# Other tokens for the first expert pass, and unsplit float32 keys for the first query tile, in a fused attention and expert kernel

## The chip, the cores and the metric

The program runs on one core of one Trainium2 chip. The metric is the device time of one execution in microseconds (us); the time before is the median of three executions. The trace is that of one profiled execution; "us" in it counts from the span's start.

## The reference

Three stages follow each other: attention with a learned relative bias, a layer of four gated experts, and a gated product layer. Cut to what matters:

```python
# q, k, v: (batch 2, heads 8, positions 576, head width 64), float32
scores = q @ k.T / 8 + bias[h, i, j]      # bias: a 1-32-8 network of log1p|i-j| / log1p(i)
attn = softmax(scores); x = attn @ v      # -> x: (1152 tokens, 512)
for e in range(4):                        # domain_probs, normalised, are the gates p
    out += p[:, e:e+1] * (relu(x @ w1[e]) @ w2[e])      # 512 -> 1024 -> 512
a = out @ w_a; b = out @ w_b              # 512 -> 1536
result = (a * b) @ w_out                  # 1536 -> 512
```

A score row of position i needs the bias rows of that position alone; the expert layer works token by token.

## The kernel before

**The order.** No instruction order is written by hand. The code declares operations with a cost on each engine, a rank and the buffers that they hold (`op`, lines 99 to 124). A planner (`Plan.run`, lines 137 to 223) plays them through with these costs and emits each engine's instructions in the order in which it would have begun them. On TensorE it prefers attention (rank 0) and fills the rest with expert products (rank 2, "fill"). On the chip every engine then runs its own list strictly in that order and waits on semaphores. All loads and stores go through SyncE's one queue, in order too.

**Precision.** Most products are done in a reduced float32 format of one TensorE pass. An operand x is split: hi is x rounded to that format, lo is x - hi. Three products hi*hi, hi*lo, lo*hi stand for one. For scores the key tile holds the same 64 rows twice, hi in partitions 0 to 63 and lo in 64 to 127 (`kcast`, `ksub`), so that two products (with qh and with ql, line 490) cover the sum. Other products (bias network, transposes, attention times values) are plain float32.

**Bias.** 36 groups of 16 positions (`bias_group`, line 347): per group three rectified tiles `hh` on VectorE (line 356) and one on ScalarE (358), four products into `pb` (370), a shift and a mirror into one of three buffers `bst` (388, 395), and a store to the DRAM table `bias_d` (405). A score step loads its 128 rows back as the tile `bt` (458), after the stores of all rows that it needs have landed.

**Attention.** The 576 positions are five query tiles t = 0 to 4 (four of 128, one of 64). A *step* is one head pair m (four of them), one batch b and one tile t, made of two *score units*, one for each head: the products `ps` (490), the sum with the bias and its row minimum on VectorE (`L493`), the exponential on ScalarE (503), transposes `pt` (516, 533), and their copies into `ptb`. A *group* is one or more steps of a head pair, closed by `values` (546): the reciprocal of the row sums, its spread `rp`, the product with the values `pv` (581), `xf` (587), and the split into `x_hi` and `x_lo`. The groups before are: tile 0 of batch 0 for each m, tile 1 of batch 0 for each m, tiles 0 and 1 of batch 1, then tiles 2 to 4 of both batches (lines 415 to 417). Keys are loaded and split by `inputs` (429) once for tiles 0 and 1 and once more for tiles 2 to 4, 16 times in all.

**Score buffers.** There are two PSUM buffers for `ps` and four for `pt`, `rp` and `pv` until the seventh group has ended (`experts_begin`, 1010). From then on there are one and two, and the others serve the experts.

**Experts.** The first pass of the experts (`w1_item`, line 724, with the products `up` of line 708; `w2_item`, 739, with `pz` of line 719) takes tokens 0 to 255 of the token order, the second pass the other 896. In each pass there are 32 weight units of 512 KB, loaded, cast and split (`unit`, 615). The first 256 tokens are batch 0's tiles 0 and 1 (`X[0, 0]`, line 730), so the first pass can begin when the first eight groups are done; the second pass begins when the attention has ended. After that come the products of the last stage (line 842), in which no part of the attention is left.

Of the kernel before, what the change touches and what calls it, by code (L numbers as in the profile page):

```python
# [19 lines left out]
P = 128  # L20
# [9 lines left out]
C0 = 256  # L30
CW = (C0, S - C0)
BW = 2 * S
# [12 lines left out]
SPLIT = True  # L45
# [181 lines left out]
def tile_kernel(ctx, tc, qd, kd, vd, cst, probs, w1r, w2r, war, wbr, wor, out):  # L227
# [56 lines left out]
    W2 = CW[1]  # L284
    place(R["q2"], ap_, "q2", 1, [P, 2, W2])
    place(R["q"], ap_, "q", 2, [P, 2, W2], F32R, pair=True)
# [4 lines left out]
    place(R["ptb"], ap_, "ptb", 2, [P, 9, W2])  # L291
    place(R["pr"], ap_, "pr", 3, [P, 2, S])
    place(R["rb"], ap_, "rb", 2, [P, W2])
    place(R["xf"], ap_, "xf", 2, [P, W2])
# [7 lines left out]
    place(R["h1"], mid, "h", 2, [P, 2, C0], F32R, pair=True)  # L302
# [116 lines left out]
    QK, fins, guests = {}, [], []  # L419
# [9 lines left out]
    def inputs(m, b, c):  # L429
        w = CW[c]  # L430
        q2, k2 = new("q2"), new("k2")
        if (b, c) == (0, 0) and m >= 2:
            d = slice(2 * m - 4, 2 * m - 2)
            k = Buf(t=x_hi[:, d, C0:C0 + S])
            q = Buf(t=tuple(x_lo[:, d, C0 + z * C0:2 * C0 + z * C0] for z in range(2)))
        else:
            k, q = new("k"), new("q")
        op({"SP": 440}, lambda e: nc.sync.dma_start(out=q2.t[:, :, :w], in_=qd[m, b][:, :, C0 * c:C0 * c + w]), w=[q2], size=P * 8 * w)
        op({"SP": 440}, lambda e: nc.sync.dma_start(out=k2.t, in_=kd[m, b]), w=[k2], size=P * 8 * S)
        op(t_copy(2 * w, ENGINES["qcast"]), lambda e: copy(e, q.t[0][:, :, :w], q2.t[:, :, :w]), r=[q2], w=[q], prio=RANK["prep"], lock=True)  # L440
        op(t_two(2 * w, ENGINES["qsub"]), lambda e: engine[e].tensor_tensor(out=q.t[1][:, :, :w], in0=q2.t[:, :, :w], in1=f(q.t[0][:, :, :w]), op=ALU.subtract), r=[q2], rw=[q], prio=RANK["prep"], lock=True)
# [27 lines left out]
    def step(m, b, t, k, q0, Q, K, ptb, sums):  # L469
# [3 lines left out]
        for s in range(2):  # L473
# [67 lines left out]
        else:  # L541
            for s in range(2):
                rr = slice(s * D, (s + 1) * D)
                op(t_psum(64, ENGINES["tail"]), lambda e, s=s, rr=rr: copy(e, ptb.t[rr, 8, 256:320], tail.t[rr, s * D:(s + 1) * D]), r=[tail], w=[ptb])

    def values(m, b, ts, w, V, ptb, sums):
# [12 lines left out]
        def spread(e):  # L559
            for t in range(full):  # L560
                nc.tensor.transpose(rp.t[:, t * P:t * P + P], rx.t[:, t].rearrange("p s d -> p (s d)"), ident)
            if 4 in ts:
                nc.tensor.transpose(rp.t[:, n:n + P], sums.t[:, 4:5].to_broadcast([P, P]), ident)
# [20 lines left out]
        c = int(ts[0] > 1)  # L584
# [532 lines left out]
```

## Time and profile before

| what | value |
|---|---|
| median of three executions | 833.38 us (832.92 to 834.51) |
| profiled execution: span from the first to the last instruction | 829.8 us |
| median less that span | 3.6 us |
| TensorE busy in the span | 802.7 us (97%) |
| VectorE busy in the span | 627.3 us (76%) |
| ScalarE busy in the span | 352.5 us (42%) |

The span is that of the profiled execution; its own time outside the span is not recorded, so the 3.6 us between it and the median of the other executions stand for what lies around it. "Busy" is the union of an engine's recorded instructions; TensorE's are pipelined and overlap, so the start of one to the start of the next is the cost in a dense stretch, not its duration. "Idle before" names what ended the idle time in front of an instruction.

### The profile page before, as it was taken

The page shows a single profiled execution, that of the slowest core. Times are in us where ns is not written, and L with a number is a line of the kernel's source. Part 1 is how long each engine was busy: PE and PEld are TensorE (multiplying, and loading weights), DVE is VectorE, ACT ScalarE, POOL GpSimd, SP SyncE. Part 2 cuts the span into 40 slices and gives each one's busy share as a digit, 9 for nine tenths or more (in the row PEclk, how much of TensorE's full clock was granted, in tenths as well). Part 3 has the DMA queues.
Part 4 walks back from the last instruction along what each step waited for, and adds up shares of the span by engine and source line. Part 5 has one row for each costly group of instructions (what it writes and reads, how often), then busy time and mean ns, then how long its engine had stood idle before and what let it go on. Part 6 is the DMA issues. An engine that isn't in the chain of part 4 may idle for free.

```text
span 829.8 us, 12737 instructions
## 1 busy us (share of the span) xinstructions
PE 802.7 (97%) x4859; PEld 668.8 (81%) x4859; DVE 627.3 (76%) x1232; ACT 352.5 (42%) x696; POOL 43.5 (5%) x62
## 2 busy tenths in 40 slices
PE   7778999999999999999999999999999999999997
PEld 2446776898897788889888988888888999899996
DVE  7998999788888768787888787875556665747545
ACT  6677877477676611132122212213345432323211
POOL 1002100000110000000000000000010001100000
PEclk9999999999999999999999999999999999999999
DMA  6989877575656444556465555640302221211103
GB/s 225 311 286 355 280 242 249 195 238 189 222 176 213 131 164 120 185 176 206 115 199 194 164 141 169 224 126 2 101 1 87 67 66 37 77 31 47 51 2 114
DMA packets 48589, 128.13 MB, mean 154 GB/s; under 512 B 5136, under 2 KB 9488, under 8 KB 48528
## 3 DMA queue, kind: packets, MB, share of 16 engines
q1 hardware_dynamic: 48384, 127.18, 47.5%
q8 instruction: 38, 0.62, 0.3%
q14 instruction: 23, 0.19, 0.1%
q10 hardware_dynamic: 144, 0.13, 0.0%
HBM read 101.46 MB, written 25.84 MB: 153 GB/s over the span
## 4 chain that ended last, share of the span: by engine, by line
PE 90%; DVE 5%; DMA 3%; ACT 1%; issue 1%; DVEq 0%
PE pz L719 32%; PE up L708 24%; PE pw L842 9%; PE ps L490 5%; PE pv L581 4%; PE pr L842 4%; PE pt L516 4%; PE pq L842 2%; PE pb L370 2%; DMA k<-in_kd 1%; DVE hh L356 1%; PE pz L922 1%; DMA bt<-bias_d 1%; ACT pr L503 1%; DMA bias_d<-bst 1%
## 5 line engine op out<-in xcount | busy, mean ns | idle before, releaser
L719 PE MATMUL pz<-wh,hh 128*128 128x512 f32 x386 | 154.0, 399 | 0.0
L719 PE MATMUL pz<-wl,hh 128*128 128x512 f32 x386 | 152.3, 395 | 0.0
L719 PE MATMUL pz<-wh,hl 128*128 128x512 f32 x386 | 151.6, 393 | 0.0
L708 PE MATMUL up<-x_hi,wh 128*128 128x256 f32 (+2 forms) x384 | 133.1, 347 | 0.4 <-DVE hl L736 0.4
L708 PE MATMUL up<-x_hi,wl 128*128 128x256 f32 (+2 forms) x384 | 129.8, 338 | 0.0
L708 PE MATMUL up<-x_lo,wh 128*128 128x256 f32 (+2 forms) x384 | 129.7, 338 | 0.0
L735 ACT ACTIVATE hh<-up 128x256 fp32r<-128x256 f32 (+2 forms) x96 | 47.1, 491 | 141.7 <-PE up L708 141.2
L234 ACT CAST wh<-wst 128x1024 fp32r<-128x1024 f32 (+1 forms) x66 | 66.4, 1007 | 91.0 <-PE pz L719 71.4
L719 PEld LDWEIGHTS pz<-wl,hh 128*128 128x128 f32 x386 | 72.5, 188 | 17.2
L619 DVE TENSOR_TENSOR wl<-wst,wh 128x1024 fp32r<-128x1024 f32 x64 | 78.0, 1222 | 9.9 <-ACT wh L234 9.6
L719 PEld LDWEIGHTS pz<-wh,hh 128*128 128x128 f32 x386 | 72.6, 188 | 15.0 <-issue 0.7
L719 PEld LDWEIGHTS pz<-wh,hl 128*128 128x128 f32 x386 | 72.6, 188 | 14.7
L708 PEld LDWEIGHTS up<-x_hi,wh 128*128 128x128 f32 x384 | 72.4, 188 | 9.5 <-issue 1.6
L708 PEld LDWEIGHTS up<-x_lo,wh 128*128 128x128 f32 x384 | 72.4, 189 | 6.5
L708 PEld LDWEIGHTS up<-x_hi,wl 128*128 128x128 f32 x384 | 72.3, 188 | 5.9
L736 DVE SCALAR_TENSOR_TENSOR hl<-up,hh 128x256 fp32r<-128x256 f32 (+2 forms) x96 | 53.0, 554 | 29.3 <-ACT hh L735 28.8
L234 ACT COPY ct<-pw 128x512 f32<-128x512 f32 (+3 forms) x48 | 27.8, 579 | 108.0 <-PE pw L842 100.6
L493 DVE CUSTOM_DVE_ANT_0 pr<-ps,bt 128x576 f32<-128x576 f32 (+1 forms) x80 | 59.7, 754 | 10.9 <-PE ps L490 8.4
L503 ACT ACTIVATE pr<-pr,sums 128x576 f32<-128x576 f32 x72 | 55.9, 776 | 12.5 <-DVE sums L493 11.7
L370 PE MATMUL pb<-hh,cs 128*32 128x288 f32 (+17 forms) x352 | 46.6, 497 | 6.6 <-DVE hh L356 5.1
L356 DVE TENSOR_SCALAR hh<-cs,negb 128x576 f32<-128x576 f32 (+17 forms) x108 | 49.1, 504 | 0.2
L516 PE MATMUL pt<-ident,pr 128*128 128x128 f32 x288 | 43.6, 280 | 2.6 <-ACT pr L503 2.4
(161 smaller groups left out, 1415.6 us busy)
## 6 DMA issues: line engine op xcount, KB each, us to landing
wst<-in_w1r SPq DMA_DIRECT2D x32, 512.0 KB, 4.1
wst<-in_w2r SPq DMA_DIRECT2D x32, 512.0 KB, 4.3
bt<-bias_d SPq DMA_DIRECT2D x24, 576.0 KB, 5.7
bias_d<-bst SPq DMA_DIRECT2D x36, 295.5 KB, 4.7
k<-in_kd SPq DMA_DIRECT2D x16, 576.0 KB, 4.9
v<-in_vd SPq DMA_DIRECT2D x20, 320.0 KB, 4.9
s<-in_war SPq DMA_DIRECT2D x12, 512.0 KB, 5.1
wz_d<-hl SPq DMA_DIRECT2D x24, 256.0 KB, 2.5
```

The costliest lines, as they stand in the source:

```text
L234: (nc.scalar.copy if e == "ACT" else engine[e].tensor_copy)(out, in_)
L356: op({"DVE": n / 1.92 + 240}, lambda e, hh=hh, G=G: nc.vector.tensor_scalar(out=hh.t[:, :n], in0=tab[:, :n], scalar1=sc[:, G:G + 1], scala ...
L370: nc.tensor.matmul(t[32 * g:32 * g + 32, o + lo:o + hi], w2s, hs[g].t[:, lo:hi], start=True, stop=True)
L493: nc.vector.tensor_tensor_reduce(out=pr.t[r0:r1, c].rearrange("p (a b) -> p a b", a=2), in0=ps.t[r0:r1, :, :HS], in1=bt.t[r0:r1, c].rearra ...
L503: nc.scalar.activation(out=pr.t[:, c], in_=pr.t[:, c], func=AF.Exp, scale=-1.0, bias=sums.t[:, neg:neg + 1], accum_out=sums.t[:, col:col + 1])
L516: nc.tensor.transpose(pt.t[:, kt * P:kt * P + P], pr.t[:, s, k0:k0 + P], ident)
L619: op(t_two(1024, ENGINES["wlo"]), lambda e: engine[e].tensor_tensor(out=w.t[1], in0=wst.t, in1=f(w.t[0]), op=ALU.subtract), r=[wst], rw=[w ...
L708: nc.tensor.matmul(u.t[:, :n], a[:, d, ft * P:(ft + 1) * P], x[:, d, lo:lo + n], start=(d == 0 and j == 0), stop=(d == 3 and j == 2))
L719: nc.tensor.matmul(z.t, a[:, ft, tt * P:(tt + 1) * P], bb[:, ft, :], start=(first and ft == 0 and j == 0), stop=(final and ft == 1 and j = ...
L735: relu = op({"ACT": n / 1.2 + 170}, lambda en, ft=ft, u=u: nc.scalar.activation(out=h.t[0][:, ft, :n], in_=u.t[:, :n], func=AF.Relu), r=[u ...
L736: op({"DVE": n / 0.96 + 160}, lambda en, ft=ft, u=u: nc.vector.scalar_tensor_tensor(out=h.t[1][:, ft, :n], in0=u.t[:, :n], scalar=0.0, in1 ...
L842: nc.tensor.matmul(o_, s[:, k], d[:, k], start=(first and k == 0 and i == 0), stop=(k == 1 and i == 2), skip_group_check=True)
```

## The change

The first 256 tokens of the token order become query tile 0 of batch 0 and query tile 0 of batch 1. The groups become: tile 0 of both batches for each m (8 groups), then for each m tiles 1 and 2 of both batches, then tiles 3 and 4 of both. For tile 0 the scores are plain float32: the keys lie in a new array `kf` once, with head width in the partitions and the two halves of the 576 positions in partitions 0 to 63 and 64 to 127, and a unit is two products, one for each half (`qk_plain`). Neither keys nor queries are cast or split there. For the other tiles keys are loaded and split once for each head pair and batch (`keys`), 8 times in all, and queries for each group (`queries`). The raw key buffer `k2` becomes two, the split key buffer `k` three.

```diff
-C0 = 256
+C0 = P
+GW = (256, 320)
+X0 = B * C0
+QW = 2 * P
...
-    place(R["k2"], ap_, "k2", 1, [P, 2, S])
-    place(R["k"], ap_, "k", 2, [P, 2, S], F32R)
+    place(R["k2"], ap_, "k2", 2, [P, 2, S])
+    place(R["k"], ap_, "k", 3, [P, 2, S], F32R)
...
-    groups = [(m, 0, (t,)) for t in range(2) for m in range(NM)] if SPLIT else [(m, 0, (0, 1)) for m in range(NM)]
-    groups += [(m, 1, (0, 1)) for m in range(NM)]
-    groups += [(m, b, (2, 3, 4)) for m in range(NM) for b in range(B)]
+    groups = [(m, b, (0,)) for m in range(NM) for b in range(B)]
+    groups += [(m, b, ts) for m in range(NM) for ts in ((1, 2), (3, 4)) for b in range(B)]
...
-    def inputs(m, b, c):
...
+    def plain(m):
+        k2, q2 = new("k2"), new("q2")
+        op({"SP": 440}, lambda e: nc.sync.dma_start(out=k2.t.rearrange("p b n -> p (b n)"), in_=kf[m]), w=[k2], size=P * 8 * S)
+        for b in range(B):
+            op({"SP": 440}, lambda e, b=b: nc.sync.dma_start(out=q2.t[:, b].rearrange("p (s w) -> p s w", s=2), in_=qd[m, b][:, :, :P]), w=[q2], size=P * 8 * P)
+        return k2, q2
+
+    def keys(m, b):
+        k2, k = new("k2"), new("k")
         op({"SP": 440}, lambda e: nc.sync.dma_start(out=k2.t, in_=kd[m, b]), w=[k2], size=P * 8 * S)
         op(t_copy(2 * S, ENGINES["kcast"]), lambda e: copy(e, k.t, k2.t), r=[k2], w=[k], prio=RANK["prep"], lock=True)
         op(t_two(2 * S, ENGINES["ksub"]), lambda e: engine[e].tensor_tensor(out=k.t[D:P], in0=k2.t[D:P], in1=f(k.t[D:P]), op=ALU.subtract), r=[k2], rw=[k], prio=RANK["prep"], lock=True)
-        return q, k
+        return k
...
+            def qk_plain(e, s=s, ps=ps):
+                for half in range(2):
+                    r = slice(half * D, half * D + D)
+                    nc.tensor.matmul(ps.t[:, half, :HS], Q.t[r, b, s * P:s * P + P], K.t[r, b, s * HS:s * HS + HS], start=True, stop=True)
+
+            op({"PE": 640}, qk_plain, r=[Q, K, bt], w=[ps], hold=[pr, sums]) if t == 0 else op({"PE": 560 if len(runs) == 2 else 700}, qk, r=[Q, K, bt], w=[ps], hold=[pr, sums])
...
-        xs = [X[0, 0]] if p == 0 else list(X.values())[1:]
+        xs = [X[b, p] for b in range(B)]
```

**Where it moves instructions.** VectorE, between the bias groups, ahead of the first score sums (`hh` are the rectified tiles, whose width falls by 16 from group to group; `k`, `x_hi` and `x_lo` are places of split keys and queries). Before:

```order
L356 TENSOR_SCALAR hh<-cs,negb 128x464 x3
L443 TENSOR_TENSOR k<-k_210,k 64x1152
L356 TENSOR_SCALAR hh<-cs,negb 128x448 x2
L234 CAST x_lo<-q_259 128x2x256
L356 TENSOR_SCALAR hh<-cs,negb 128x448
L441 TENSOR_TENSOR x_lo<-q_259,x_lo 128x2x256
L356 TENSOR_SCALAR hh<-cs,negb 128x432 x3
```

The changed kernel:

```order
L357 TENSOR_SCALAR hh<-cs,negb 128x464 x3
L357 TENSOR_SCALAR hh<-cs,negb 128x448 x3
L357 TENSOR_SCALAR hh<-cs,negb 128x432 x3
L357 TENSOR_SCALAR hh<-cs,negb 128x416 x3
L357 TENSOR_SCALAR hh<-cs,negb 128x400 x3
```

Every cast and split of keys and queries has left this stretch; the first score sum follows the same 42 `hh` tiles as before.

TensorE, around the first expert product `up`. Before, where 22 score units stand ahead of it:

```order
L581 MATMUL pv<-ptb,v 64x128 x10
L516 MATMUL pt<-ident,pr 128x128 x4
L533 MATMUL pt<-ident,pr 128x128
L490 MATMUL ps<-k,qh 128x288 x2
L490 MATMUL ps<-k,ql 128x288 x2
L561 MATMUL rp<-ident,rx 128x128 x2
L370 MATMUL pb<-hh,cs 32x400 x4
L490 MATMUL ps<-k,qh 128x288 x2
L490 MATMUL ps<-k,ql 128x288 x2
L708 MATMUL up<-x_hi,wh 128x256
```

The changed kernel, where 18 units stand ahead (16 of tile 0, two of tile 1):

```order
L371 MATMUL pb<-hh,cs 32x320 x4
L589 MATMUL pv<-ptb,v 64x128 x10
L524 MATMUL pt<-ident,pr 128x128 x4
L371 MATMUL pb<-hh,cs 32x336 x4
L524 MATMUL pt<-ident,pr 128x128 x4
L541 MATMUL pt<-ident,pr 128x128
L589 MATMUL pv<-ptb,v 64x128 x10
L371 MATMUL pb<-hh,cs 32x352 x4
L722 MATMUL up<-x_hi,wh 128x256
```

The expert products now come after the products of 22 bias groups instead of 25, and 36 of them stand in a row there.

TensorE, where the first expert pass ends (`pz` is its second product; `up` of 384 columns is the second pass). Before:

```order
L719 MATMUL pz<-wl,hh 128x512
L516 MATMUL pt<-ident,pr 128x128 x4
L535 MATMUL pt<-ident,pr 128x128
L536 MATMUL pt<-ident,pr 64x128
L561 MATMUL rp<-ident,rx 128x128 x2
L563 MATMUL rp<-ident,sums 128x128
L581 MATMUL pv<-ptb,v 64x320 x10
L708 MATMUL up<-x_hi,wh 128x384
```

The changed kernel:

```order
L733 MATMUL pz<-wl,hh 128x512
L495 MATMUL ps<-k,qh 128x288 x2
L495 MATMUL ps<-k,ql 128x288 x2
L524 MATMUL pt<-ident,pr 128x128 x4
L543 MATMUL pt<-ident,pr 128x128
L544 MATMUL pt<-ident,pr 64x128
L495 MATMUL ps<-k,qh 128x288 x2
L495 MATMUL ps<-k,ql 128x288 x2
L569 MATMUL rp<-ident,rx 128x128
L571 MATMUL rp<-ident,sums 128x128
L524 MATMUL pt<-ident,pr 128x128 x4
```

Before, one `pv` is left to do after the last `pz` of the first pass; now 20 of the 80 score units, with their transposes and six `pv`, come after it. From the first `up` of 384 columns on, TensorE's two lists are the same.

## Rows read from the trace of the kernel before

**Rows 1.** The page's head, and its busy time by engine.

```profile
span 829.8 us, 12737 instructions
PE 802.7 (97%) x4859; PEld 668.8 (81%) x4859; DVE 627.3 (76%) x1232; ACT 352.5 (42%) x696; POOL 43.5 (5%) x62
```

**Rows 2.** Stretches: length, busy us by engine (instructions), clock, DMA share, GB/s.

```profile
0.00:31.39 31.39, 23.03 (x136) 6.46 (x136) 25.79 (x54) 20.10 (x30) 4.01 (x15) 1.00 0.72 232
31.39:80.00 48.61, 39.00 (x346) 27.36 (x345) 45.83 (x130) 36.18 (x82) 4.23 (x5) 0.96 0.95 337
...
91.33:279.00 187.67, 187.23 (x1375) 153.73 (x1374) 161.21 (x328) 130.53 (x276) 12.68 (x15) 1.00 0.66 212
279.00:293.84 14.84, 13.36 (x90) 8.77 (x88) 9.88 (x20) 8.51 (x20) 0.88 (x1) 1.00 0.41 136
```

**Rows 3.** The line of the expert products: shortest, median, longest ns; first and last start.

```profile
L708 PE MATMUL up<-x_hi,wh x384: 277/336/481, 91.3 to 596.7; 128*128 128x256 f32 x64, 128*128 128x384 f32 x64, 128*128 128x512 f32 x64
```

**Rows 4.** VectorE by line, 4.2 to 33.4 us: busy, mean ns, idle before.

```profile
L356 DVE TENSOR_SCALAR hh<-cs,negb 128x576 f32<-128x576 f32 (+13 forms) x42 | 19.4, 521 | 0.1
L443 DVE TENSOR_TENSOR k<-k,k 64x1152 fp32r<-64x1152 f32 x2 | 2.7, 1355 | 1.4 <-ACT k L234 1.3
L441 DVE TENSOR_TENSOR ql<-q,qh 128x512 fp32r<-128x512 f32 x2 | 1.4, 686 | 0.0
L234 DVE CAST qh<-q 128x512 fp32r<-128x512 f32 x2 | 0.8, 424 | 0.0
L234 DVE CAST x_hi<-k 128x1152 fp32r<-128x1152 f32 x1 | 0.8, 759 | 0.2 <-DMA k<-in_kd 0.2
```

**Rows 5.** SyncE's queue in order of time: start, length, transfer, count.

```profile
22.12 1.39 SPq L405 DMA_DIRECT2D bias_d<-bst  x2
27.96 0.89 SPq L458 DMA_DIRECT2D bt<-bias_d  x2
```

**Rows 6.** Transfers issued from 8 to 32 us: size, median us to landing.

```profile
bias_d<-bst SPq DMA_DIRECT2D x10, 295.5 KB, 4.1
bt<-bias_d SPq DMA_DIRECT2D x3, 576.0 KB, 5.1
```

**Rows 7.** VectorE in order of time: start, length, instruction, idle before.

```profile
33.43 0.74 DVE L493 CUSTOM_DVE_ANT_0 pr<-ps,bt 128x576 f32<-128x576 f32 x1
34.10 0.08 DVE L493 DVE_READ_ACCUMULATOR2_ANT sums<- 128x1 f32 x1
...
35.06 0.76 DVE L493 CUSTOM_DVE_ANT_0 pr<-ps,bt 128x576 f32<-128x576 f32 x1 [0.21 <-PE ps L490]
...
36.71 0.67 DVE L234 COPY ptb<-pt 128x512 f32<-128x512 f32 x1
...
43.98 1.20 DVE L356 TENSOR_SCALAR hh<-cs,negb 128x352 f32<-128x352 f32 x3
...
46.08 1.22 DVE L619 TENSOR_TENSOR wl<-wst,wh 128x1024 fp32r<-128x1024 f32 x1
...
65.66 0.76 DVE L493 CUSTOM_DVE_ANT_0 pr<-ps,bt 128x576 f32<-128x576 f32 x1 [1.56 <-DMA bt<-bias_d]
```

**Rows 8.** TensorE in order of time, early, and the values' product of a long group.

```profile
38.71 1.31 PE L490 MATMUL ps<-x_hi,x_lo 128*128 128x288 f32 x8
39.95 1.31 PE L581 MATMUL pv<-ptb,v 128*64 128x128 f32 x20
...
45.09 1.42 PE L370 MATMUL pb<-hh,cs 128*32 128x368 f32 x16
...
280.20 2.91 PE L581 MATMUL pv<-ptb,v 128*64 128x320 f32 x20
```

**Rows 9.** TensorE in order of time, the attention's end.

```profile
288.73 0.66 PE L516 MATMUL pt<-ident,pr 128*128 128x128 f32 x4 [0.43 <-ACT pr L503]
...
290.52 0.44 PE L561 MATMUL rp<-ident,rx 128*128 128x128 f32 x2 [0.91 <-ACT ptb L234]
...
293.84 0.44 PE L708 MATMUL up<-x_hi,wh 128*128 128x384 f32 x1
```

More of the change, by code (lines that the diff above doesn't have):

```diff
@@ L226, in tile_kernel @@
 @with_exitstack
-def tile_kernel(ctx, tc, qd, kd, vd, cst, probs, w1r, w2r, war, wbr, wor, out):
+def tile_kernel(ctx, tc, qd, kd, kf, vd, cst, probs, w1r, w2r, war, wbr, wor, out):
     nc = tc.nc
@@ L301, in tile_kernel @@
     place(R["wst"], right, "wst", 2, [P, 1024])
-    place(R["h1"], mid, "h", 2, [P, 2, C0], F32R, pair=True)
+    place(R["h1"], mid, "h", 2, [P, 2, X0], F32R, pair=True)
     new = lambda z, name=None: Buf(R[z], None, name or z)
@@ L442, in inputs, with queries @@
         op(t_copy(2 * S, ENGINES["kcast"]), lambda e: copy(e, k.t, k2.t), r=[k2], w=[k], prio=RANK["prep"], lock=True)
         op(t_two(2 * S, ENGINES["ksub"]), lambda e: engine[e].tensor_tensor(out=k.t[D:P], in0=k2.t[D:P], in1=f(k.t[D:P]), op=ALU.subtract), r=[k2], rw=[k], prio=RANK["prep"], lock=True)
-        return q, k
+        return k
+    def queries(m, b, lo, w):
+        q2, q = new("q2"), new("q")
+        z = lambda t: t.rearrange("p s w -> p (s w)")[:, :2 * w]
+        op({"SP": 440}, lambda e: nc.sync.dma_start(out=z(q2.t).rearrange("p (s w) -> p s w", s=2), in_=qd[m, b][:, :, lo:lo + w]), w=[q2], size=P * 8 * w)
+        op(t_copy(2 * w, ENGINES["qcast"]), lambda e: copy(e, z(q.t[0]), z(q2.t)), r=[q2], w=[q], prio=RANK["prep"], lock=True)
+        op(t_two(2 * w, ENGINES["qsub"]), lambda e: engine[e].tensor_tensor(out=z(q.t[1]), in0=z(q2.t), in1=f(z(q.t[0])), op=ALU.subtract), r=[q2], rw=[q], prio=RANK["prep"], lock=True)
+        return q
@@ L467, in bias_tile, with step @@
         return bt
-    def step(m, b, t, k, q0, Q, K, ptb, sums):
+    def step(m, b, t, k, q0, Q, qw, K, ptb, sums):
         bt = bias_tile(m, t)
@@ L543, in step @@
                 rr = slice(s * D, (s + 1) * D)
-                op(t_psum(64, ENGINES["tail"]), lambda e, s=s, rr=rr: copy(e, ptb.t[rr, 8, 256:320], tail.t[rr, s * D:(s + 1) * D]), r=[tail], w=[ptb])
+                op(t_psum(64, ENGINES["tail"]), lambda e, s=s, rr=rr: copy(e, ptb.t[rr, 8, q0:q0 + D], tail.t[rr, s * D:(s + 1) * D]), r=[tail], w=[ptb])
     def values(m, b, ts, w, V, ptb, sums):
@@ L562, in spread @@
             if 4 in ts:
-                nc.tensor.transpose(rp.t[:, n:n + P], sums.t[:, 4:5].to_broadcast([P, P]), ident)
+                nc.tensor.transpose(rp.t[:, n:n + P], sums.t[:, 2 * full:2 * full + 1].to_broadcast([P, P]), ident)
         def spread_copy(e):
@@ L588, in values @@
         hi = Buf(t=x_hi)
-        op(t_copy(w, ENGINES["xhi"]), lambda e: copy(e, x_hi[:, m, o], xf.t[:, :w]), r=[xf], w=[hi], prio=RANK["fin"], lock=True, after=guests if (b, c) != (0, 0) else ())
+        op(t_copy(w, ENGINES["xhi"]), lambda e: copy(e, x_hi[:, m, o], xf.t[:, :w]), r=[xf], w=[hi], prio=RANK["fin"], lock=True)
         fins.append(op(t_two(w, ENGINES["xlo"]), lambda e: engine[e].tensor_tensor(out=x_lo[:, m, o], in0=xf.t[:, :w], in1=f(x_hi[:, m, o]), op=ALU.subtract), r=[xf, hi], w=[X[b, c]], prio=RANK["fin"], lock=True))
     def group(m, b, ts):
-        c = int(ts[0] > 1)
-        if (m, b, c) not in QK:
-            QK[m, b, c] = inputs(m, b, c)
+        w = min(P * ts[-1] + P, S) - P * ts[0]
+        if ts[0] == 0:
+            if m not in QK:
+                QK[m] = plain(m)
+            K, Q = QK[m]
+        else:
+            if (m, b) not in QK:
+                QK[m, b] = keys(m, b)
+            K, Q = QK[m, b], queries(m, b, P * ts[0], w)
         V, ptb, sums = new("v"), new("ptb"), new("sums")
@@ L598, in group @@
         for k, t in enumerate(ts):
-            step(m, b, t, k, P * k, *QK[m, b, c], ptb, sums)
-        values(m, b, ts, sum(P if t < 4 else D for t in ts), V, ptb, sums)
+            step(m, b, t, k, P * k, Q, w, K, ptb, sums)
+        values(m, b, ts, w, V, ptb, sums)
     CHUNKS = ((0, 2), (2, 3), (5, 4))
@@ L765, in xb @@
             if c == 0:
-                xb_t[c, z] = late["xb"].tile([P, 7, 2, CW[0]], F32R, name=f"xb{z}")
+                xb_t[c, z] = late["xb"].tile([P, 7, 2, GW[0]], F32R, name=f"xb{z}")
             else:
-                xb_t[c, z] = (x_hi, x_lo)[z].rearrange("p k n -> p (k n)")[:, :14 * CW[1]].rearrange("p (j k n) -> p j k n", j=7, k=2)
+                xb_t[c, z] = (x_hi, x_lo)[z].rearrange("p k n -> p (k n)")[:, :14 * GW[1]].rearrange("p (j k n) -> p j k n", j=7, k=2)
         return xb_t[c, z]
@@ L942, in out_item @@
                 op({"SP": 440 * len(rows_of(t))}, put, r=[ACC[t]], size=262144)
-    QK[0, 0, 0] = inputs(0, 0, 0)
+    QK[0] = plain(0)
     op({"PE": 600}, corr_mm, r=[cs], w=[pc])
@@ L1003, in first_end @@
         for i in range(2):
-            R["sum"].add(lambda name, i=i: tuple(mid.tile([P, 2, C0], F32, tag=f"h{i}{z}", name=f"{name}{z}", bufs=1) for z in "hl"))
+            R["sum"].add(lambda name, i=i: tuple(mid.tile([P, 2, X0], F32, tag=f"h{i}{z}", name=f"{name}{z}", bufs=1) for z in "hl"))
     def converted_end():
         cv_stack.close()
-        place(R["ct"], tp(ctx, "ct"), "ct", 2, [P, 4, 2, W2])
+        place(R["ct"], tp(ctx, "ct"), "ct", 2, [P, 4, 2, GW[1]])
     def experts_begin():
```

42 lines of the change are left out of this document (13 added, 29 removed).

## The prediction

> **What bounds the kernel now.** I read the page's busy times first: TensorE is busy for 802.7 of 829.8 us [rows 1], so only 27.1 us of its idle time and a change in its own work are there to be won. The table of stretches says where that idle time lies: 8.4 us before 31.39, 9.6 us from there to 80, 0.4 us up to 279 and 1.5 us in the 14.8 us up to 293.84 [rows 2]. In the first 80 us VectorE is the full engine (45.83 of 48.61 us in the second stretch), while TensorE has only attention and bias to do. The expert products, which fill TensorE's gaps, start at 91.3 [rows 3]. From there to 293.84, where the second expert pass starts [rows 9], attention and first pass share a TensorE that is full. From that instruction on its two lists are the same, so I take the 536 us behind it as unchanged, and the whole question is when that instruction starts. It starts when three things add up: the start of the first expert product, TensorE's work from there, and the idle time in between. For before that is 91.3 + 200.6 + 1.9 = 293.8 (the work is 202.5 us less idle times of 0.44 and 1.48 [rows 2]).
>
> **The bias stage.** Ahead of the first score sum at 33.43 [rows 7] VectorE does 42 bias tiles in 19.4 us, and between them four query casts (0.42 each), four query subtractions (0.69), three key subtractions (1.36) and a key cast (0.76) [rows 4]: 9.3 us, all gone. But the first sum also needs its bias tile. Its load was issued at 27.96, after the eighth store, which was issued about 23 [rows 5]; a store takes 4.1 us to land and the load 5.1 [rows 6]. Of the removed work 3.6 us stood before the eighth group's tiles, and ScalarE's side of that group also waited behind a key cast; I put the eighth store at 18.5, its landing at 22.6 and the load's at 27.7. VectorE has its 42 tiles by 4.2 + 19.4, about 24, so the bias tile, not VectorE, now comes last: some 4 us of the 9.3 turn into a wait. First sum at 27.7. Bounds: 26, if stores land in less than the median as few loads run beside them, and 31, if the three `bst` buffers, each held for side, mirror, issue and landing (about 5.5 us for three groups of 1.4 us on VectorE), pace the stage.
>
> **From the first sum to the first expert product.** In the changed order VectorE has, from that sum to the last piece of x that the first expert pass needs: 18 sums at 0.68 (33.43 to 34.10) = 12.2; 27 bias tiles at some 0.37 (three in 1.20, overlapping) = 9.8; four weight subtractions at 1.14 (1.22 less overlap) = 4.6 [rows 7]; three key casts and key subtractions, now for tile 1, at 0.70 + 1.36 = 6.2 and two for queries at 0.4 + 0.6 = 2.0 [rows 4]. The rest are some 45 small ones, from 0.15 for a piece of x to 0.6 for a 512-wide copy out of PSUM [rows 7]; I count 11.3. Sum 46.1. VectorE idled for 2.8 us in the 48.6 us of the like stretch before [rows 2], 1.6 of them in the wait for tile 1's bias at 65.66 [rows 7], which no longer stands ahead of the experts; I add 1.5. The first expert product starts at 27.7 + 46.1 + 1.5 = 75.3, 16 us sooner. Bounds: 72 and 82.
>
> **What plain float32 costs there.** A unit of four split products takes 0.63 (eight in 1.31 are two units [rows 8]). No row shows a product of 64 rows. The nearest are plain products on column strips. Ten of the values, five pairs on two strips, go from 1.31 to 2.91 when 128 columns become 320: 1.67 ns a column for each pair, four clocks at 2.4 GHz. Four strips of the bias, 368 columns, take 0.71 [rows 8], and 368 times 1.67 is 0.61: four strips cost what two do, so they run at once. If two row halves do so too, a unit costs 288 * 1.67 = 0.48 plus some 0.05: 0.53. In turn they cost 1.0. I take 0.53, nearest to the strips; 16 units make 8.5 or 16 us. By these prices TensorE has, from the first sum to the first expert product, 81 transposes at 0.14 (a little under a quarter of the 0.66 that four take with their latency [rows 9]; 11), eight values' products (10.5), ten bias groups (7), the units (9.8 with two of tile 1) and the spreads (1): 39 us in a stretch of 47.6. Even 46.5 would just fit.
> The Trainium skill speaks on both sides. "TensorE: Matmul & The Clock Gate" (Part 3, packing small matmuls) says that tiles in different row groups run concurrently, by which the unit is 0.53, and the trace has that for column strips only. "TensorEngine Tiling (Array Packing)" (Key Properties) says that a change of tiling mode drains the engine, which speaks against the change, since tile 0's units put such changes between the transposes. What the trace has of it is small: the ten products of 128 columns cost 0.24 more than their columns [rows 8], changes of mode included, and 16 times that would be 3.9 us, in the same slack.
>
> **TensorE's work behind the first expert product.** Fewer instructions stand ahead of it, so more come after: four score units (2.5), nine transposes at 0.14 (1.2), two spreads (0.3) and three bias groups (2.4). Products with the values grow from 20 groups to 24 with the same columns in all; between 128 and 320 columns the price goes from 1.31 to 2.91 [rows 8], so a group has a fixed 0.24, 1.0 in all. The work is 200.6 + 7.4 = 208.0.
>
> **The end of the attention.** The first pass has the same 32 weight units, begun 16 us sooner against an attention that ends late, so its products run out while 20 score units are to come; in before they lasted to the end, with idle times of 0.43 and 0.91 in front of the last transposes and spread [rows 9]. In this tail there is one score buffer. A unit then cannot follow sooner than its own 0.63, 0.2 to reach VectorE, 0.7 for the sum (0.75 with its read-out) and a hand-over [rows 7, 8]: 1.6 us. TensorE's work of the tail is 37.9 us, 1.9 a unit, but uneven: 14 gaps between units hold only transposes and leave 0.2 to 0.4 idle each, and six hold the values' product of 1.8 to 2.4. That makes about 4 us, and the last chain of sum, exponential, transposes, copies and spread another 2: 6 us against 1.5. Bounds: 3 and 12.
>
> **The rest.** Eight full bias loads and four key loads of 576 KB go, four value loads of 320 KB come, and SyncE's queue has about as many entries as before; the engines of the DMA had a share of 0.95 up to 80 us and 0.66 behind [rows 2], so this only loosens the first stretch, which stands in the bounds. Eight key casts and subtractions (2.1 us each [rows 4]) go from VectorE and ScalarE; most of it lies beside a full TensorE and is worth nothing while first-pass products last. In the dense fill behind 75 us TensorE uses a weight unit in about 4.5 us; I add 0.5 for a late weight or bias tile.
>
> **Sum.** 75.3 + 208.0 + 6 + 0.5 = 289.8, 4.0 us before 293.8. The span becomes 825.8. The median of the runs shown, 833.38, lies 3.6 us above the span of the profiled execution, and with the same distance the time is 829.4 us. Alone, this case goes from 826 to 832.
>
> **Rivals.**
> *The tail eats it (slower).* The experts' start is early, but the 20 units behind their end are paced by the one score buffer and the exponential, not by TensorE's 1.9 us. It decides at a tail idle time of 293.8 - 75.3 - 208.0 - 0.5 = 10.0, that is 2.4 us a unit; at 2.6 the tail idles for 14 us and the time is 837.4. For it: even with filling products the end of before idled for 1.5 us. Against: the chain of one buffer is 1.6 us. Chance 0.21.
> *The bias stage does not move.* Stores and the loads behind them pace it, and the first sum comes at 31 to 32 instead of 27.7: nothing is left, 833. For it: of 9.3 us removed I already give 4 to the wait. Against: VectorE was busy for nearly all of 4.2 to 33.4. Chance 0.12.
> *Plain float32 is dear.* Row halves in turn, or drains: 4 to 7.5 us more in a stretch with some 8 us to spare; in strict order perhaps 3 of it shows: 832.4, no difference that can be told. Chance 0.10.
> *More is won.* Stores land fast, the experts start at 72.5, and the tail idles for 3 us: 284.0, time 823.6. Chance 0.13.
> *The forecast:* 0.44.
>
> **How the numbers follow.** A measurement of this kernel can tell about 0.2%, 1.7 us, from no change. Faster are the forecast and the large gain, 0.57; the two middle rivals make 0.22 for no difference; slower 0.21. The range of 8 in 10 leaves out the far ends of the tail rival and of the large gain: 823 to 836.5.
>
> **What would show it.** In the profile after: the first score sum near 28 with an idle time on VectorE ahead of it that a bias load ends; the first 256-column expert product near 75; a TensorE that is full from there on; the last first-pass `pz` some 44 us before the first product of 384 columns, and between them 4 to 8 us of idle time ended by VectorE's sums and ScalarE's exponentials; 536 us from that product to the end. The prediction is wrong if the first sum stays at 31 or later, if tile 0's units take 1 us and TensorE, not VectorE, is full ahead of the experts, or if the tail idles for more than 10 us.

## The result and the profile after

The changed kernel takes 839.7 us (median of four executions, 838.86 to 841.73) against 833.15 us for the kernel before beside it: a ratio of 1.0079, with a 95% interval of 1.0063 to 1.0095. It is slower by 6.6 us. The forecast was 829.4 us, faster. In the executions that have both numbers the time is some 1.8 us more than the span (838.86 and 837.1 for the profiled one here). So the 3.6 us that were taken for what lies around the span before are 1.8 of that, and 1.8 by which the profiled execution of before was quicker than the median; by the spans the loss is 7.3 us.

The page's head and busy times answer to [rows 1]:

```profile
span 837.1 us, 12913 instructions
PE 804.8 (96%) x4939; PEld 670.1 (80%) x4939; DVE 618.3 (74%) x1250; ACT 340.1 (41%) x678; POOL 52.1 (6%) x74
```

The table of stretches of the changed kernel, with the columns of [rows 2], cut where the forecast cut: at the first score sum, the first expert product, the end of the last first-pass `pz`, and the first product of the second pass; two shorter stretches ahead of the first expert product stand between:

```profile
0.00:25.72 25.72, 18.58 (x144) 7.15 (x144) 19.01 (x47) 19.07 (x32) 4.01 (x14) 1.00 0.71 250
25.72:77.04 51.32, 43.49 (x394) 27.15 (x394) 47.72 (x134) 37.63 (x83) 7.60 (x13) 0.93 0.94 325
...
64.68:70.37 5.69, 1.31 (x20) 1.07 (x21) 5.63 (x10) 1.32 (x4) 0.77 (x1) 0.93 0.92 328
70.37:77.04 6.67, 6.67 (x46) 4.03 (x46) 4.55 (x13) 3.47 (x7) 0.40 (x1) 0.55 0.89 304
...
77.04:255.59 178.55, 174.64 (x1290) 142.13 (x1287) 145.69 (x304) 110.02 (x228) 16.45 (x19) 1.00 0.65 204
255.59:301.18 45.59, 39.31 (x306) 30.06 (x304) 33.22 (x97) 26.06 (x69) 4.54 (x6) 1.00 0.35 109
301.18:837.10 535.92, 528.81 (x2813) 463.64 (x2811) 372.63 (x669) 147.36 (x267) 19.46 (x22) 1.00 0.34 108
```

The reader is to see four things. The first sum came at 25.72 and the first expert product at 77.04, 14.3 us sooner than the 91.3 of [rows 3]. The second pass started at 301.18, 7.3 us later than the 293.84 of [rows 9]. What follows takes 535.9 us, as long as before, so the whole loss lies between 77 and 301 us. And there TensorE looks busy: 174.6 of 178.6 us, then 39.3 of 45.6.

TensorE of the changed kernel in order of time, with the columns of [rows 8]: plain score units, the stop ahead of the experts, three waits in the filled stretch, and the end of the attention:

```profile
31.80 1.24 PE L513 MATMUL ps<-k,q 64*128 64x288 f32 x8
32.97 0.85 PE L371 MATMUL pb<-hh,cs 128*32 128x384 f32 x8
...
64.68 1.31 PE L589 MATMUL pv<-ptb,v 128*64 128x128 f32 x20 [0.26 <-DMA v<-in_vd]
70.37 1.12 PE L524 MATMUL pt<-ident,pr 128*128 128x128 f32 x4 [4.38 <-ACT pr L508]
...
73.96 2.40 PE L589 MATMUL pv<-ptb,v 128*64 128x128 f32 x20
...
141.69 0.53 PE L495 MATMUL ps<-k,qh 128*128 128x288 f32 x2 [0.90 <-DVE sums L498]
...
151.49 0.39 PE L722 MATMUL up<-x_hi,wh 128*128 128x256 f32 x1 [1.11 <-DVE hl L750]
...
158.77 0.39 PE L722 MATMUL up<-x_hi,wh 128*128 128x256 f32 x1 [0.93 <-DVE hl L750]
...
288.76 0.53 PE L495 MATMUL ps<-k,qh 128*128 128x288 f32 x2 [0.32 <-DVE sums L498]
289.13 0.42 PE L495 MATMUL ps<-k,ql 128*128 128x288 f32 x2
289.82 0.66 PE L524 MATMUL pt<-ident,pr 128*128 128x128 f32 x4 [0.27 <-ACT pr L508]
...
297.46 0.66 PE L524 MATMUL pt<-ident,pr 128*128 128x128 f32 x4 [1.33 <-ACT pr L508]
297.95 0.27 PE L543 MATMUL pt<-ident,pr 128*128 128x128 f32 x1
298.06 0.27 PE L544 MATMUL pt<-ident,pr 128*64 128x128 f32 x1
299.04 0.33 PE L569 MATMUL rp<-ident,rx 128*128 128x128 f32 x1 [0.70 <-DVE ptb L236]
```

**A ledger.** "Busy" hides part of the loss, since a product that fills a gap alone shows its whole latency as busy time. So I price each of TensorE's instructions between the first expert product and the second pass by what it took, start to start, in the filled stretch of the kernel before (91.33 to 288.15): 248 score products in 34.5 us (0.139 each), 240 transposes in 23.4, 384 `up` in 49.4, 192 `pz` in 45.8, 27 spreads in 2.9; bias and values' products at what they took. The time by which a stretch is longer than that sum is its waste, idle time and exposed latency together. All kernels of this study, in us of the profiled execution; "tail" is what lies behind the last first-pass `pz`, and "left" the score products in it (four to a unit, six in some):

| kernel | first `up` | priced work | waste, filled | waste, tail | left | second pass |
|---|---|---|---|---|---|---|
| before | 91.3 | 200.0 | 0.6 | 1.9 | 0 | 293.8 |
| changed | 77.0 | 206.3 | 5.6 | 12.2 | 86 | 301.2 |
| e1_tiles_first | 79.1 | 206.1 | 10.2 | 3.1 | 18 | 298.5 |
| e2_bias_first | 76.8 | 206.8 | 7.8 | 3.7 | 24 | 295.0 |
| e3_split_tile0 | 79.0 | 211.0 | 7.9 | 11.4 | 74 | 309.3 |
| e4_two_score_buffers | 81.3 | 206.2 | 5.2 | 7.5 | 86 | 300.2 |
| e5_even_fill | 78.5 | 207.1 | 4.7 | 0.1 | 0 | 290.4 |
| e6_order_bias | 80.0 | 208.1 | 5.3 | 5.9 | 28 | 299.3 |
| e7_bias_two_buffers | 77.9 | 206.3 | 7.9 | 3.2 | 24 | 295.4 |
| e8_before_even | 102.4 | 193.2 | 3.6 | 0.1 | 0 | 299.4 |
| e9_even_split0 | 78.3 | 211.6 | 8.6 | 0.1 | 0 | 298.5 |
| e10_margin_only | 80.7 | 206.3 | 5.9 | 8.7 | 56 | 301.6 |
| e11_bias_margin | 80.2 | 208.4 | 2.9 | 10.2 | 68 | 301.6 |

The changed kernel against the one before: the start is worth -14.3, the work behind it +6.3, the waste in the filled stretch +5.0 and in the tail +10.3; the sum is +7.3 us. In e8_before_even 12 of the `pz` follow the start of the second pass, so its last column stands some 2.9 us too low beside the others.

Each row is one execution, and the early part of it varies. Up to the tail, e4_two_score_buffers has the changed kernel's own instruction lists on every engine, and yet its first expert product came 4.3 us later. Its first score sum, the first plain units behind it, and the stretch from there to its first expert product:

```profile
28.15 0.76 DVE L498 CUSTOM_DVE_ANT_0 pr<-ps,bt 128x576 f32<-128x576 f32 x1 [5.10 <-DMA bt<-bias_d]
28.97 2.29 PE L513 MATMUL ps<-k,q 64*128 64x288 f32 x8 [4.95 <-DVE sums L498]
28.15:81.31 53.16, 45.33 (x394) 28.02 (x394) 47.99 (x134) 37.81 (x83) 7.62 (x13) 0.87 0.91 312
```

Its bias tile ended a longer wait (5.10 us against 2.87 in the changed kernel), TensorE stood for 4.95 us, and two plain units behind that took 2.29 us instead of the 1.24 us that they take at 31.80 in the changed kernel; the granted clock up to the first expert product was 0.87 instead of 0.93. So differences of up to some 4 us in the second column need not come from an edit. The mean granted clock of a whole execution goes from 0.990 to 1.000 over all runs, and long times go with low clocks: e11_bias_margin took 839.22 us at 0.990, which is its profiled execution, and 832.18 at 0.998.

### The profile page after: what moved, and what is told of

Same layout as the page of the kernel before. It is cut to its first block, busy times and chain, and to the rows that moved or that the text cites. A ratio compares the mean times of both kernels' runs of the same rounds, so it can differ in the third digit from the quotient of the medians.

```text
span 837.1 us, 12913 instructions
## 1 busy us (share of the span) xinstructions
PE 804.8 (96%) x4939; PEld 670.1 (80%) x4939; DVE 618.3 (74%) x1250; ACT 340.1 (41%) x678; POOL 52.1 (6%) x74
## 4 chain that ended last, share of the span: by engine, by line
PE 87%; DVE 7%; ACT 2%; DMA 2%; issue 1%; POOL 0%; DVEq 0%; SPq 0%; ACTq 0%; POOLq 0%
PE pz L733 31%; PE up L722 23%; PE pw L856 9%; PE pv L589 4%; PE pr L856 4%; PE ps L495 4%; PE pt L524 3%; PE pb L371 3%; PE pq L856 2%; DVE pr L498 2%; DVE k L440 1%; PE pz L936 1%; PE ps L513 1%; DVE hh L357 1%; DVE ptb L236 1%
## 5 line engine op out<-in xcount | busy, mean ns | idle before, releaser
L236 ACT CAST wh<-wst 128x1024 fp32r<-128x1024 f32 (+1 forms) x61 | 61.3, 1005 | 89.4 <-PE pz L733 70.6
L633 DVE TENSOR_TENSOR wl<-wst,wh 128x1024 fp32r<-128x1024 f32 x64 | 77.9, 1220 | 14.3 <-ACT wh L236 13.6
L498 DVE CUSTOM_DVE_ANT_0 pr<-ps,bt 128x576 f32<-128x576 f32 (+1 forms) x80 | 59.8, 753 | 10.3 <-PE ps L495 6.0
L236 ACT COPY ptb<-pt 128x512 f32<-128x512 f32 (+3 forms) x78 | 34.3, 470 | 29.3 <-PE pt L524 27.4
```

The costliest lines, as they stand in the source:

```text
L236: (nc.scalar.copy if e == "ACT" else engine[e].tensor_copy)(out, in_)
L498: nc.vector.tensor_tensor_reduce(out=pr.t[r0:r1, c].rearrange("p (a b) -> p a b", a=2), in0=ps.t[r0:r1, :, :HS], in1=bt.t[r0:r1, c].rearra ...
L633: op(t_two(1024, ENGINES["wlo"]), lambda e: engine[e].tensor_tensor(out=w.t[1], in0=wst.t, in1=f(w.t[0]), op=ALU.subtract), r=[wst], rw=[w ...
```

## The experiments

The first theory was "hole". In the changed order the 25th score unit already needs tile 3's bias and the 27th tile 4's, and between 120 and 160 us VectorE makes three score sums, while the filling products run out. The rival was "one score buffer".

**e1_tiles_first.** Tiles 1 and 2 of everything ahead of tiles 3 and 4, for keys split twice:

```diff
-    groups += [(m, b, ts) for m in range(NM) for ts in ((1, 2), (3, 4)) for b in range(B)]
+    groups += [(m, b, ts) for ts in ((1, 2), (3, 4)) for m in range(NM) for b in range(B)]
...
-            if (m, b) not in QK:
-                QK[m, b] = keys(m, b)
-            K, Q = QK[m, b], queries(m, b, P * ts[0], w)
+            K, Q = keys(m, b), queries(m, b, P * ts[0], w)
```

> The changed kernel with its last 16 groups in another order: tiles 1 and 2 of every head pair and batch first, tiles 3 and 4 after them, the keys of a head pair and batch split once for each of the two (16 splits again instead of 8). Theory 'hole': with the order of the changed kernel the attention needs tile 3's and tile 4's bias from its 25th score unit on, long before the last bias groups are made, so it does hardly anything between 120 and 160 us, uses up the filling expert products there, and 20 units are left over for the tail. Then this order fills the hole: 4 to 5 units in the tail instead of 20, first expert product still near 77 us, second pass at 288 to 291 us instead of 301.2, time 827 to 830 us. Theory 'split once': the gain of the change sits in the eight saved key splits, and VectorE and ScalarE with eight more of them hold up the filled stretch; then the time stays at 838 or more.

Measured: 838.73 us, 1.0077 (1.0059 to 1.0095). The two stretches behind its first expert product, in the table of stretches:

```profile
79.12:284.99 205.87, 201.00 (x1493) 163.42 (x1490) 176.34 (x375) 139.95 (x291) 25.56 (x22) 1.00 0.65 208
284.99:298.49 13.50, 11.89 (x105) 8.91 (x103) 10.83 (x28) 7.34 (x23) 0.00 (x0) 1.00 0.58 168
```

The tail shrank from 45.6 to 13.5 us, as the theory said, but the time lies far above its 827 to 830 and cannot be told from the changed kernel's. The waste had moved: 10.2 us in the filled stretch. Between 120 and 160 us this kernel does 16 units beside only some 7 us of expert products, and wastes some 5 us there. "Hole" is therefore not enough. The time is in the range that "split once" gave (838 or more), but that theory falls later: e5_even_fill splits the keys as often as this run and is the fastest of all. What the two places have in common is attention without expert products beside it. That became the second theory, "cover": filling products cover the waits and latencies of attention, and each score unit that runs without them costs TensorE some 0.6 us (12.2 us for 86 products, four to a unit).

**e2_bias_first.** One number:

```diff
-RANK = {"prep": 0.5, "bias0": 0, "bias1": 0.6, "bias2": 1, ...
+RANK = {"prep": 0.5, "bias0": 0, "bias1": 0.6, "bias2": 0, ...
```

> The changed kernel with the rank of the bias groups behind tile 1 put from 1 to 0, so that they go as early as attention does; groups and key splits stay as changed. Theory 'hole': the last bias group comes after some 29 us of filling products instead of 39, 6 units are left for the tail instead of 20, second pass near 291 us instead of 301.2, time 828 to 832 us. Rival 'one score buffer': units in the tail and units in the filled stretch are paced alike by the single score buffer and the chain behind it, and moving them between the two is worth under 2 us: 838 or more.

Measured: 833.45 us, 1.0008 (0.9997 to 1.0019). 24 score products were left, and the second pass started at 295.0, 6.2 us sooner. One number gave nearly the whole loss back, though the time lies above the range of 828 to 832. The second pass still came 4 us later than this run's forecast had it, since the filled stretch wasted 7.8 us.

**e3_split_tile0.** Without the plain scores:

```diff
-            if m not in QK:
-                QK[m] = plain(m)
-            K, Q = QK[m]
+            K, Q = QK.pop((m, b, 0), None) or (keys(m, b), queries(m, b, 0, w))
...
-            op({"PE": 640}, qk_plain, r=[Q, K, bt], ...) if t == 0 else op({"PE": 560 ...}, qk, ...)
+            op({"PE": 560 ...}, qk, r=[Q, K, bt], w=[ps], hold=[pr, sums])
```

> The changed kernel with the plain float32 scores undone: tile 0 uses keys and queries that are cast and split as for the other tiles (eight more splits, order of tokens and groups as changed). If the plain scores give the early start, the first score sum goes back from 25.7 to 30 to 33 us and the first expert product from 77.0 to 86 to 90 us. What it costs in time: by the theory that an early start is worth its full length, 9 to 12 us more (849 to 852); by the theory that the attention behind is the bound and the start is lost again in the tail, at most 4 us more (842 to 844).

Measured: 847.4 us, 1.0175 (1.0154 to 1.0197), between the two theories. Its first two stretches:

```profile
0.00:34.41 34.41, 22.18 (x152) 7.28 (x152) 25.71 (x57) 24.20 (x38) 9.54 (x15) 1.00 0.74 248
34.41:79.01 44.60, 36.85 (x329) 28.05 (x329) 43.07 (x113) 32.09 (x73) 8.04 (x12) 0.94 0.81 271
```

The first sum went back by 8.7 us, but the first expert product by 2.0 only, not by 9 or more: the order puts five bias groups and two score units behind it instead. Those stand in the ledger as 4.7 us more work. So the plain scores are worth 7.7 us, and the rest of the change (token order and groups) costs 847.4 - 832.8 = 14.6 us against the kernel before. This run splits keys 16 times, as often as the kernel before, so the 7.7 us hold the eight splits that tile 0 does without.

**e4_two_score_buffers.** A second score buffer in the tail, in the idle banks of `up`:

```diff
+    tail = ExitStack()
     def first_end():
+        if not all(o.done for o in fins):
+            del R["u"].free[:]
+            stacks[0].close()
+            place(R["s"], tp(tail, "ps_c", space=PSUM, side="right"), "s", 1, [P, 2, 512], mark="tail")
...
     def attn_end():
+        R["s"].retire("tail")
+        tail.close()
+        place(R["u"], tp(stacks[0], "ps_u2", space=PSUM, side="right"), "u2", 2, [P, 512], mark="u")
```

> The changed kernel with a second score buffer in the tail: when the first expert pass has run out, the two PSUM banks of its idle up buffers serve the scores until the attention ends. Rival 'one score buffer': the tail of 45.6 us shrinks by 4 to 7 us, since the next unit's products no longer wait for the sum of the one before; time 833 to 836 us. Theory 'chain': what the tail loses is lost in the chain of sum, exponential, transposes, copies and values' product and in TensorE's exposed latencies, and only the 2 us of waits for sums are to be had: 837.5 to 839.5 us.

Measured: 836.07 us, 1.0034 (1.0018 to 1.0051). Its tail:

```profile
259.40:300.15 40.75, 37.35 (x307) 29.86 (x305) 30.93 (x93) 28.08 (x76) 2.63 (x3) 1.00 0.40 122
```

4.8 us shorter than 45.59 with the same work, at a granted clock of 1.00 in both: the one buffer is 4.7 of the tail's 12.2 us of waste. TensorE's waits for score sums fell from 2.3 us in the tail to 0.2. The other 7.5 us of waste stay with two buffers, so they are put down to the chain and the exposed latencies. Both theories hold a share.

**e5_even_fill.** The edits of e1_tiles_first and e2_bias_first, and one number more:

```diff
-QUICK, BY_AGE, MARGIN, LATE = 0.9, True, 300, True
+QUICK, BY_AGE, MARGIN, LATE = 0.9, True, 0, True
```

> The changed kernel with three settings: tiles 1 and 2 of all groups ahead of tiles 3 and 4 (as in e1_tiles_first), bias rank 0 (as in e2_bias_first), and no 300 ns head start for the filling products on TensorE (MARGIN 0), by which the order keeps filling products until the attention has ended: no score unit is left for the tail. Theory 'cover': what the change lost is lost wherever attention runs without filling products beside it (12.2 us in the tail of 45.6 us, 2 to 3 us for 20 us with under 4 us of fill), so with the fill spread out the idle and exposed time behind the first expert product falls from 17.8 us to 4 to 7, the second pass starts at 288 to 291 us, and the time is 826 to 829 us, below both kernels. Rival 'paid anyway': the waste moves into the filled stretch as it did in e1_tiles_first (10.2 us there), and the time is 832 or more.

Measured: 828.0 us, 0.9936 (0.9912 to 0.996), faster than both kernels, though its mean granted clock (0.991 to 0.997) was not above theirs. Behind its first expert product:

```profile
78.51:288.50 209.99, 208.61 (x1581) 171.94 (x1579) 180.62 (x383) 147.14 (x323) 27.66 (x30) 0.99 0.65 213
288.50:290.38 1.88, 1.88 (x22) 1.35 (x21) 1.58 (x2) 1.02 (x1) 0.00 (x0) 1.00 0.40 150
```

The reader is to see that filling products last to within 1.9 us of the second pass, and that TensorE is idle for 1.4 us in 210. The waste is 4.8 us instead of 17.8, and the priced work is the same within 0.8 us. "Paid anyway" falls, and with it "split once".

**e6_order_bias.** e5_even_fill with MARGIN at 300.

> The same without the change of MARGIN: tiles 1 and 2 first and bias rank 0. Seven units are left for the tail instead of none. Theory 'cover': between e5_even_fill and e2_bias_first, waste 8 to 11 us, 831 to 834 us. Rival 'paid anyway': as e5_even_fill within 2 us.

Measured: 837.03 us, 1.0049 (1.0026 to 1.0072), a miss. The waste, 11.2 us, is near what was expected; but the first expert product came 1.5 us later than in e5_even_fill, the priced work was 1.0 us more, and in its tail the granted clock was 0.92 over 22.0 us. "Paid anyway" is refuted here again: 9 us lie between the two.

**e7_bias_two_buffers.** The edits of e2_bias_first and e4_two_score_buffers.

> The changed kernel with bias rank 0 and the second score buffer in the tail (e2_bias_first and e4_two_score_buffers together). The tail has 6 units; a second buffer took 4.7 of 12.2 us from a tail of 20, so it should take 1 to 2 us here: 831.5 to 832.5 us, about 1 us under the kernel before. If the two gains were to add in full, 830.

Measured: 833.47 us, 1.0006 (0.9988 to 1.0024). The second buffer took 0.5 us of waste from a tail of 24 products, less than expected, and nothing of the time that can be told; the time lies above the range of 831.5 to 832.5.

**e8_before_even.** The two numbers in the kernel before: bias rank 0 and MARGIN 0.

> The kernel before with the same two numbers as e5_even_fill (bias rank 0 and MARGIN 0; its order of groups has tiles 2 to 4 last anyway). Theory 'cover': its waste behind the first expert product was only 2.5 us, so there is nothing for them to win, and bias groups ahead of attention move the first expert product back: 833 to 838 us. Rival: the two numbers are simply better in any kernel, and it gains as much as e5_even_fill does against the changed kernel, 5 us or more: 828 or less.

Measured: 839.38 us, 1.0082 (1.006 to 1.0103). The first expert product went back by 11.1 us to 102.4, and there was little waste to win. The time lies above the 833 to 838 expected, and the rival (828 or less) falls. So the two numbers are no gain by themselves: what wins together with the change and its tile order loses in the kernel before.

**e9_even_split0.** e5_even_fill with the split keys of e3_split_tile0.

> e5_even_fill with split keys and queries for tile 0, as in e3_split_tile0, so without the plain float32 scores. In the changed kernel the plain scores were worth 7.7 us, although the first expert product started only 2.0 us sooner with them: the rest was 4.7 us of TensorE work ahead of it instead of behind it (five bias groups, minus two score units) and 1.5 us of waste. None of the three has to do with the tail, so with the fill spread out they are worth the same: 835 to 837 us. Rival: what the plain scores win is only that the attention ends sooner, which an even fill makes worthless: 829 to 831 us.

Measured: 837.54 us, 1.0059 (1.0036 to 1.0082), half a microsecond above the range. Without the plain scores the even fill loses 9.5 us: in the profiled executions 4.5 us of work that no longer stands ahead of the experts, and 3.9 us of waste; the rest is not accounted for. The rival falls.

**e10_margin_only** and **e11_bias_margin.** MARGIN 0 alone, and MARGIN 0 with bias rank 0, both in the order of the changed kernel.

> The changed kernel with MARGIN 0 alone; groups and bias ranks as changed. 14 score units are left for the tail instead of 20. Theory 'cover': the waste in the tail goes with the units left for it (20 units 12.2 us, 7 units 5.9, 6 units 3.7, 4.5 units 3.1), so 14 units cost some 8.5 us, and the time is 835 to 838 us. Rival: the head start of the filling products itself costs the time, by waits at each hand-over, and taking it away gives most of what e5_even_fill gave: 829 to 831 us.

> Bias rank 0 and MARGIN 0 with the groups in the order of the changed kernel, so e5_even_fill without its order of tiles, or e2_bias_first with MARGIN 0. 17 units are left for the tail, against 6 in e2_bias_first and none in e5_even_fill. Theory 'cover': worse than e2_bias_first though it differs by a setting that helped elsewhere: tail waste near 10 us, 836 to 840 us. Rival: each of the settings helps by itself, and two of three give 829 to 833 us.

Measured: 838.25 us, 1.0061 (1.0034 to 1.0089), and 836.46 us, 1.0027 (1.0008 to 1.0047). Their tails, of the first and of the second:

```profile
267.86:301.57 33.71, 29.03 (x231) 22.04 (x229) 22.82 (x68) 18.42 (x46) 2.05 (x3) 1.00 0.31 99
```

```profile
262.61:301.62 39.01, 34.04 (x252) 25.37 (x250) 25.97 (x80) 21.60 (x54) 3.94 (x5) 0.96 0.31 96
```

Tail wastes of 8.7 and 10.2 us were forecast as 8.5 and near 10. The first run's time lies a quarter of a microsecond above its range, the second's inside. e11_bias_margin differs from e2_bias_first only by the setting that e5_even_fill needs; its median is 3 us higher, but the two intervals overlap (1.0008 to 1.0047 and 0.9997 to 1.0019) and part of its tail ran at a lower clock (0.96 over the 39 us). Neither rival came (829 to 831 and 829 to 833). Over the changed kernels with one score buffer the tail wastes 0.57 to 0.84 us for each four products left (with two, 0.35 and 0.53), and 0.1 us for none.

## Why the prediction was wrong

**Right.** VectorE bounds the stage ahead of the experts, and the removed key work turns partly into a wait for the bias tile. VectorE of the changed kernel, with the columns of [rows 7]:

```profile
25.72 0.76 DVE L498 CUSTOM_DVE_ANT_0 pr<-ps,bt 128x576 f32<-128x576 f32 x1 [2.87 <-DMA bt<-bias_d]
...
66.13 1.36 DVE L440 TENSOR_TENSOR k<-k,k 64x1152 fp32r<-64x1152 f32 x1
67.52 1.23 DVE L633 TENSOR_TENSOR wl<-wst,wh 128x1024 fp32r<-128x1024 f32 x1
68.66 0.75 DVE L498 CUSTOM_DVE_ANT_0 pr<-ps,bt 128x576 f32<-128x576 f32 x1
```

The wait for the bias tile was 2.9 us instead of some 4, the first sum at 25.7 instead of 27.7, just beyond the lower bound of 26. "The bias stage does not move" falls. 536 us from the second pass to the end: 535.9.

**Plain float32.** Two units took 1.17 us from start to start (31.80 to 32.97), 0.59 each, against 0.53 taken and 1.0 in turn: the two row halves run at once (the trace's records of one such pair start at 51.021 and 51.028), and that rival falls. The Trainium skill ("TensorE: Matmul & The Clock Gate", Part 3, packing small matmuls) says so of tiles in different row groups, and the trace agrees by that 0.59. A unit alone between transposes takes 0.69. The Trainium skill ("TensorEngine Tiling (Array Packing)", Key Properties) says that a change of tiling mode drains TensorE; this trace shows 0.1 us more a unit where a unit stands alone than in a run of two, and no run tells a drain there from exposed latency.

**The first expert product** came at 77.0, forecast 75.3. Its stage took 51.3 us, not 47.6. VectorE was busy for 47.7, near the 46.1 + 1.5; the rest is a cost that the forecast did not have. At 66 to 68.7 VectorE is still on keys and weights, while the sums of tile 1 stand behind them; TensorE waits 4.38 us for the exponential that follows those sums, its granted clock falls, and in the 6.67 us from 70.37 on it is 0.55: a values' product takes 2.40 instead of 1.31. TensorE is busy throughout and VectorE waits for it. By an estimate, some 0.45 * 6.67 = 3 us went there. The kernel before had such a stretch too, at 66.90 to 70.30 with a granted clock of 0.50, some 1.7 us by the same estimate. e4_two_score_buffers shows how far this start varies with one and the same list.

**The step that failed is "TensorE's work behind the first expert product"**, which carries the 20 units of the tail at the prices of a stretch with filling products. In the forecast's own terms of busy and idle time, the 11.4 us between 289.8 and 301.2 are:

| term | forecast | measured | difference |
|---|---|---|---|
| first expert product | 75.3 | 77.0 | +1.7 |
| TensorE's work from there (busy) | 208.0 | 174.64 + 39.31 = 213.95 | +5.9 |
| idle time in the tail | 6 | 6.3 | +0.3 |
| idle time ahead of the tail | 0.5 | 3.9 | +3.4 |

At the ledger's prices the work was right: 206.3 us, 6.3 more than before where 7.4 was said. "The end of the attention" was near, too: 20 units were left, as counted, the tail took 45.6 us against 43.9 (37.9 of work and 6 idle), and its idle time came out at 6.3. What the sum put at nothing is the busy time that a tail adds. At filled prices its work is 33.4 us, and TensorE was busy for 39.3: without filling products its own latencies show, 5.9 us, as busy time beside the idle time. A transpose took 0.13 us from start to start there, idle time left out, against 0.097 in the filled stretch, and a score product 0.17 against 0.139. I had most of this in the tail's own 37.9 (1.9 us a unit, against 1.67 at filled prices), but I left the 208.0 as it was. Ahead of the tail another 1.7 us of latency show as busy time, as much as the forecast's work was above the ledger's 206.3.

**The second failure is "The rest"**: half a microsecond for late weights and bias tiles became 3.9 us of idle time, 5.6 us of waste. 2.9 of it are the three waits at 141.69, 151.49 and 158.77. VectorE of the changed kernel ahead of them:

```profile
139.74 1.23 DVE L633 TENSOR_TENSOR wl<-wst,wh 128x1024 fp32r<-128x1024 f32 x1 [3.72 <-ACT wh L236]
...
149.88 1.23 DVE L633 TENSOR_TENSOR wl<-wst,wh 128x1024 fp32r<-128x1024 f32 x1 [1.70 <-ACT wh L236]
...
157.15 1.23 DVE L633 TENSOR_TENSOR wl<-wst,wh 128x1024 fp32r<-128x1024 f32 x1 [0.47 <-ACT wh L236]
```

Ahead of each wait, VectorE's list has one of these weight splits in front of the sum or the `hl` (the low half of a hidden tile) that TensorE waited for, and the split stood until ScalarE's cast was there. Attention stood nearly still at this time: between 116.2 and 158.96 there are two score sums, at 140.88 and 142.82, and tile 4's bias tile was loaded from 151.63 on, behind the last bias store at 148.01. That the one led to the other is argued, not shown. What the remaining 2.7 us are is open, and so is why this waste is 2.9 us in e11_bias_margin and 7.8 in e2_bias_first.

"The tail eats it" was the rival nearest to the result in direction and time (837.4), but not for its reason. It decides at 10.0 us of idle time in the tail, and there were 6.3. Its one score buffer is 4.7 us of the tail's waste by e4_two_score_buffers; without these the second pass would have started near 296.5, still behind 293.8. So the outcome that it named came in part by luck, through busy time in the tail and waste in the filled stretch that it did not have either. None of the three signs of being wrong came (a first sum at 31 or later, units of 1 us, a tail idle for more than 10): the last of them counts idle time alone, and the largest part of what was missed shows as busy time.

That the loss comes from attention running without filling products is shown by e5_even_fill: same plain scores, same tokens first, priced work within 0.8 us, keys split more often, with the filling products spread to the end, and the waste falls by 13 us and the time to 828.0. e10_margin_only and e11_bias_margin, whose tail wastes were forecast from the units left alone, bear out the dependence. How the waste in the filled stretch divides stays open.

## What to carry to other kernels

Work that can run at any time is cover for work that runs in a chain: in this kernel starting it 14.3 us sooner won nothing, because it no longer reached to the chain's end. Count what is left of the chain when the cover runs out, and price that stretch from a stretch without cover, not from a dense one. A planner's setting that suits one order (here the head start of the filling products, and the bias's rank) has to be chosen again when the order changes: the same two numbers cost the kernel before 6 us and, with the tile order, won the changed one 12.

## What the runs showed of the hardware

A 64-row plain float32 pair on two row halves, 288 columns, costs 0.59 us in a run of two and 0.69 alone, about as much as four split products on 128 rows (0.56 in the filled stretch). A stop of TensorE of 4.4 us at one place was followed by 6.7 us at a granted clock of 0.55, which is mostly the lower of its levels, 1.2 GHz; by the row of that stretch some 3 us were lost behind a stop of 4.4, an estimate. In e4_two_score_buffers a stop of 4.95 us, in the changed kernel's own list, was followed by two plain units that took 2.29 us instead of 1.24.
